# A gated attention and MLP kernel on one core: all steps in a new hand-written order

## The chip, the cores and the metric

The kernel runs on one core of one Trainium2 chip. The metric is device time in microseconds (us). Before the change the median of 3 runs is 445.13 us (444.56 to 445.13).

## What is computed

The output mixes two branches of one input `x` of 2048 rows and 512 columns with a gate per row:

```python
x = A_x
g = _sigmoid((x * gate_w).sum(-1, keepdims=True))
a = _A_ref(x, A_wqkv, A_w_phi, A_wo)
b = _B_ref(x, B_w1, B_b1, B_w2)
return g * a + (1 - g) * b
```

Branch A is linear attention with 32 heads of 16 columns. Queries and keys go through a small matrix per head, then through two softmaxes over the 16 columns (of the value and of its negative), which gives 32 features per head; `kv` is the sum over rows of features of the key times value, `z` the sum of the key features, and the result is `phi_q kv / (phi_q z + 1e-6)`, followed by the matrix `wo`. Branch B is `mish(x w1 + b1) w2` with 1376 hidden columns. All of it is in 32-bit floats; the big products are made of a rounded high part and a low rest (`h` and `l` in the names), three matmuls instead of one.

## The kernel before

The work is cut into steps, each a small Python function filed under a key and a name. The long string `RUN` (line 42) lists all steps, and `run` (L218) calls them in that order. Every instruction is pinned to the program's order, so each engine, and each DMA queue with it, executes its instructions in exactly the order in which the steps stand in `RUN`. An engine that waits for another holds up all that stands behind it on that engine.

The steps have three kinds of keys.

- `A0` to `A7` are eight chunks of 256 rows, of two tiles of 128 rows each. `k`, `q`, `v` and `p1` to `p7` are TensorE products into PSUM (`proj`); for each key tile VectorE takes maximum and minimum per head (`mx`, `mn`, L275), subtracts them (`d0` L285, `d1` L287, into the tile `E`), ScalarE takes the exponential (`E`), VectorE sums (`S`, L291), inverts (`rS`, L299) and scales (`ml`, L302). `kv` (L491) adds to the key-value sums on TensorE and reads `E`. Projected queries are written to DRAM (`st`, tensor `pqd`), and `z` adds up the key features. Behind chunk 7, `zt` and `zf` (L848 to L856) add up `z` across partitions (`zacc`, `zr`); `zs` (L859) writes it to DRAM and `zl` (L863) reads it back, spread over all partitions, as `zb`.
- `S0` and `S1` are the two halves of 1024 rows for the first MLP product. Pairs of hidden tiles are computed with seven products (`p1_n` to `p7_n`, tensor `up`) in place of eight; VectorE forms sums of the weights (`ws`, L687 to L690) and combines the products (`a2` L740, `a3` L743, `a7` L746); ScalarE applies mish (`mA`, `mB`).
- `B0` to `B3` are four blocks of 512 rows. `lq` reads projected queries from `pqd` into one of three `pq` buffers; each of four tiles gets the same softmax features (`mx mn d0 d1 E S rS`), then `T` (L954) multiplies `E` by `zb`, `D` (L958) sums, `m` (L977), `de` (L962), `rd` (L979) and `sc` (L966) make the factor, `es` (L302) scales `E` by it, and `tr` (L969) transposes and stores to DRAM. `mv` reads it back, `nu` multiplies by the key-value sums (`num`), `oh` on ScalarE and `ol` on VectorE (L1012) split the result, `wo` multiplies by the output matrix, `dn` and `df` are the second MLP product (`down`), and `fi` (L1061) mixes and stores.

All matmuls are issued through one helper (`mm`, L118 in the profile), and all activations through another (L138). GpSimd computes the low parts `l` and some sums. ScalarE holds one table of functions at a time; the exponential and mish lie in different tables, and a step `pm` loads the mish table ahead of need.

Of the kernel before, what the change touches and what calls it, by code (L numbers as in the profile page):

```python
# [66 lines left out]
    B0.de0 B0.rd0 S0.p7_2 B0.lo3 B0.hi4 S0.wd_3 B0.sc0 S0.sB1_1 B0.d13 S0.p2_3 B0.es0 S0.a3_2 S0.mB0_2 S0.gl3 S0.c1_3 B1.mn0 S0.sB0_2 S0.a7_2 B0.dn3
    B0.es1 B0.tr1 S0.p6_3 S0.a2_3 S0.p5_3 S0.p4_2 B0.tr0 S0.lg4 B0.lo4 B0.E3 B0.E2 B0.dn4 S0.wa_4 S0.wb_4 S0.p1_4 S0.mA1_2 B1.mx1 B0.T2 S0.c5_3 B0.hi5
    S0.c6_3 B0.lo5 S0.gh4 B0.dn5 B0.D2 B0.S3 B0.rS3 S0.ws_4 B0.T3 B0.D3 S0.p7_3 B0.mv0 B0.hi6 B0.lo6 B1.d10 B1.d00 B0.m3 S0.p2_4 S0.mB1_2 B0.S2
    S0.a7_3 S0.p3_3 S0.a3_3 S0.mA0_3 B0.hi7 S0.wc_4 B1.E0 S0.wd_4 B1.T0 S0.fr1 S0.fh1 B0.dn6 S0.mB1_3 S0.mB0_3 B1.mn1 B0.rS2 B0.m2 S0.n12 S0.p4_3  # L70
    S0.c1_4 S0.sB1_2 B0.de3 B0.lo7 B1.lq2 S0.sB1_3 S0.p5_4 B0.de2 S0.p6_4 B1.D0 B1.d01 S0.mA1_3 S0.h12 S0.a2_4 S0.fl1 B1.mx2 S0.mA0_4 B0.dn7 S0.c6_4
    B0.rd3 S0.p7_4 B0.gl S0.c5_4 B0.rd2 B0.sc2 B0.hi9 B0.hi8 S0.ldo1 S0.p3_4 S0.WH1 B0.sc3 B1.d11 B0.es3 B0.es2 S0.a7_4 S0.sB0_3 S0.o12 S0.uf1 B1.S0
    B0.lo8 B0.dn8 B0.lo9 S0.ldo0 S1.l11 B1.lq3 B0.tr2 B1.E1 B1.S1 B1.mx3 B1.la3 S0.mB1_4 B1.rS1 B1.mn3 B2.lq1 B1.mi0 S0.WL1 B0.tr3 B1.gr S0.a3_4
    S0.p4_4 B1.mn2 S0.WH0 B0.nu0 B0.oh0 S0.gl4 B1.gl B0.dn9 S0.mA1_4 B0.hi10 B0.ol0 B1.rS0 S0.WL0 B0.wo0 B1.hi0 B1.T1 B0.lo10 B1.m0 B0.ge B1.lo0 B1.D1
# [1160 lines left out]
```

## Time and profile before

| | |
|---|---|
| median of 3 runs | 445.13 us |
| the profiled execution's own time | 447.22 us |
| its span, first to last instruction | 445.5 us |
| mean granted TensorE clock | 0.992 |
| busy in the span | PE 427.9, PEld 342.7, DVE 383.1, ACT 258.0, POOL 258.9 us |
| instructions in the span | 7567 |

PE is TensorE, PEld its weight loads, DVE VectorE, ACT ScalarE, POOL GpSimd, SP the engine that issues most DMAs. Matmuls overlap in the profile: a 512-column matmul is listed with about 392 ns, and such matmuls start every 0.23 us when nothing holds them. PE's busy time therefore says little of how much work is left out; the waits, and the time between starts, say more. The two numbers 447.22 and 445.13 are different executions: durations in the text are of the profiled one.

### The profile page before, as it was taken

To read this page: it belongs to the slowest core of one execution; us is meant where nothing else is said; L and a number is where in the kernel's file an instruction comes from. 1 tells how busy PE (TensorE), PEld (TensorE's weight loads), DVE (VectorE), ACT (ScalarE), POOL (GpSimd) and SP (SyncE) were. 2 spreads that over 40 slices of the span, in tenths; PEclk is the share of its full clock that TensorE was granted. 3 is DMA by queue.
4 is the path that set the end of the run, shared out by engine and by line. 5 is a ranking of instruction groups with operands and counts; after the bars stand their busy time and mean duration, and the time that the engine had idled before them with its cause. 6 is when DMAs were issued, how large, how long until landed. Compare 5 with 4: busy or idle time off the path is not lost.

```text
span 445.5 us, 7567 instructions
## 1 busy us (share of the span) xinstructions
PE 427.9 (96%) x2778; PEld 342.7 (77%) x2778; DVE 383.1 (86%) x516; ACT 258.0 (58%) x376; POOL 258.9 (58%) x181
## 2 busy tenths in 40 slices
PE   8999999999999898999799999899999999899996
PEld 7888888888886686778578787688788887678775
DVE  3979798999998988999999999848998799999613
ACT  2556454454546678568588733278595877942331
POOL 2267967887686558476584775475383573641320
PEclk9999999999999899999999999899999999999999
DMA  7804676577985424617656587823343483627552
GB/s 261 307 25 142 167 174 147 153 153 178 232 169 146 143 84 154 200 71 224 187 197 198 190 293 210 270 76 95 96 165 96 150 229 135 173 68 248 169 179 96
DMA packets 52669, 74.06 MB, mean 166 GB/s; under 512 B 8084, under 2 KB 32148, under 8 KB 52632
## 3 DMA queue, kind: packets, MB, share of 16 engines
q1 hardware_dynamic: 50440, 66.36, 46.0%
q0 software_dynamic: 1904, 6.82, 9.1%
q10 hardware_dynamic: 288, 0.39, 0.3%
q8 instruction: 22, 0.36, 0.3%
q14 instruction: 15, 0.12, 0.1%
HBM read 43.53 MB, written 28.85 MB: 162 GB/s over the span
## 4 chain that ended last, share of the span: by engine, by line
PE 59%; DVE 27%; DMA 6%; issue 3%; ACT 2%; SPq 2%; DVEq 0%; ACTq 0%
PE proj L118 26%; PE up L118 15%; PE down L118 10%; PE wo L118 5%; DVE E L302 3%; DVE E L285 3%; DVE T L954 2%; DVE Sm L291 2%; DVE E L969 2%; DVE Dn L977 2%; DMA pq<-pqd 2%; DVE Dn L958 2%; PE kvp L118 2%; DMA wT<-in_wkT_dram 1%; DVE mx L275 1%
## 5 line engine op out<-in xcount | busy, mean ns | idle before, releaser
L118 PE MATMUL down<-w2g,h 128*128 128x512 f32 x316 | 98.4, 392 | 0.0
L118 PEld LDWEIGHTS down<-w2g,h 128*128 128x128 f32 x316 | 58.6, 188 | 14.9 <-issue 2.3
L118 PE MATMUL down<-w2g,l 128*128 128x512 f32 x158 | 61.7, 391 | 1.3 <-POOL l L824 1.3
L824 POOL TENSOR_TENSOR l<-act,h 128x512 fp32r<-128x512 f32 (+1 forms) x24 | 35.4, 1478 | 45.1 <-ACT h L138 20.9
L824 POOL TENSOR_TENSOR l<-actb,h 128x512 fp32r<-128x512 f32 x20 | 26.8, 1344 | 38.9 <-ACT h L138 22.0
L118 PE MATMUL wo<-woh,ohl 128*128 128x512 f32 x128 | 42.6, 399 | 2.6 <-DVE ohl L1012 2.4
L118 PE MATMUL up<-x,w1sh 128*128 128x512 f32 x144 | 39.4, 396 | 5.8 <-ACT act L138 3.1
L138 ACT ACTIVATE E<-E 128x1024 f32<-128x1024 f32 x32 | 33.7, 1057 | 11.8 <-DVE E L285 4.8
L118 PEld LDWEIGHTS up<-x,w1sh 128*128 128x128 f32 x144 | 26.7, 188 | 13.0 <-ACT act L138 4.0
L118 PEld LDWEIGHTS down<-w2g,l 128*128 128x128 f32 x158 | 29.7, 188 | 8.5 <-POOL l L824 2.2
L267 POOL TENSOR_TENSOR xl<-xraw,xh 128x512 fp32r<-128x512 f32 x14 | 19.5, 1452 | 22.9 <-ACT xh L138 19.8
L302 DVE TENSOR_TENSOR E<-E,Sm 128x1024 f32<-128x1024 f32 x18 | 32.1, 1788 | 0.2
L700 POOL TENSOR_TENSOR w1sl<-w1r,w1sh 128x1024 fp32r<-128x1024 f32 x9 | 22.8, 2533 | 15.6 <-ACT w1sh L138 12.1
L118 PEld LDWEIGHTS wo<-woh,ohl 128*128 128x128 f32 x128 | 24.5, 192 | 8.6 <-DVE ohl L1012 2.8
L118 PE MATMUL up<-x,w1d 128*128 128x512 f32 x108 | 27.4, 392 | 2.4 <-DVE act L740 1.8
L138 ACT ACTIVATE h<-actb 128x512 fp32r<-128x512 f32 x20 | 12.6, 629 | 29.1 <-DMA actb<-ab 20.0
L138 ACT ACTIVATE act<-act,b1s 128x512 f32<-128x512 f32 x30 | 21.1, 717 | 13.9 <-DVE act L740 6.9
L628 POOL TENSOR_TENSOR x<-xr,x 128x1024 fp32r<-128x1024 f32 x10 | 24.6, 2464 | 6.6 <-ACT x L138 6.6
L954 DVE TENSOR_TENSOR T<-E,zb 128x1024 f32<-128x1024 f32 x16 | 25.2, 1578 | 3.0 <-DMA zb<-zd 1.7
L118 PE MATMUL proj<-tw,sx 128*128 128x512 f32 x108 | 27.3, 393 | 0.3 <-ACT v L138 0.3
L138 ACT ACT_TABLE_LOAD x21 | 26.9, 1283 | 0.3
L291 DVE TENSOR_REDUCE Sm<-E 128x64 f32<-128x1024 f32 x18 | 21.5, 1197 | 5.7 <-ACT E L138 5.7
(174 smaller groups left out, 1097.5 us busy)
## 6 DMA issues: line engine op xcount, KB each, us to landing
ed<-E SPq DMA_DIRECT2D x16, 512.0 KB, 2.8
eT<-ed SPq DMA_DIRECT2D x64, 128.0 KB, 3.4
za<-E POOLq DMA_DIRECT2D x11, 512.0 KB, 5.7
xr<-in_xT_dram SPq DMA_DIRECT2D x20, 256.0 KB, 4.3
ab<-act SPq DMA_DIRECT2D x20, 256.0 KB, 2.8
actb<-ab SPq DMA_DIRECT2D x20, 256.0 KB, 3.4
pqd<-qs SPq DMA_DIRECT2D x16, 256.0 KB, 2.9
pq<-pqd SPq DMA_DIRECT2D x16, 256.0 KB, 3.5
```

The costliest lines, as they stand in the source:

```text
L118: return pin(nc.tensor.matmul(*a, **k))
L138: return pin(A_.activation(out_, in_, fn, **k))
L267: pin(eng.tensor_sub(xs[c][1][j], kt(rawx[c], SC)[:, 2 * j : 2 * j + 2, :], f32(xs[c][0][j])))
L285: pin(V.tensor_sub(E, hv(src()), d["mx"][:, :, None].to_broadcast([P, H, DH])))
L291: pin(V.tensor_reduce(d["S"], hv(d["E"][:, :]), axis=AX.X, op=ALU.add))
L302: pin(eng.tensor_mul(hv(d["E"][:, :]), hv(d["E"][:, :]), d["S"][:, :, None].to_broadcast([P, 2 * H, DH])))
L628: pin((V if n in LOV else G_).tensor_sub(X[n][:, 1024:], xr[n], f32(X[n][:, :1024])))
L700: pin(G_.tensor_sub(W["sl"], W["r"], f32(W["sh"])))
L824: pin(G_.tensor_sub(U[i]["l"][:n, :], U[i]["a"][:n, :], f32(U[i]["h"][:n, :])))
L954: pin(V.tensor_mul(d["T"], d["E"], B["zb"]))
L958: pin(V.tensor_reduce(d["D"], hv(d["T"][:, :]), axis=AX.X, op=ALU.add))
L969: pin(V.transpose(d["E"][:, :], d["E"][:, :]))
```

## The change

Only the string `RUN` changes: the same steps stand in a new order. It was searched with a replay of the program, in four cases: durations as traced, longer operations, later landings of transfers. No step is added or removed. The mish loads `pm` stand at other places (5 of them before, 1 now), and with the order of exponentials and mish activations the number of table loads on ScalarE goes from 27 to 20. The other engines execute the same instructions in another order. The first two lines of the string show the form:

```diff
-    A0.ldx A2.lx A0.mn0 A0.fq A0.fh1 A0.tA1 A0.fh0 A0.fl0 A0.mx1 A0.tA0 A2.ldx A0.fh2 A0.tB1 A0.fl1 A0.mn1 A0.d10 A0.xh A0.d11 A0.v0 A0.xl A0.tB0
-    A0.v1 A0.fl2 A0.tH1 A1.v1 A0.d01 S0.l11 A0.mx0 A0.d00 A0.tH2 A0.tL2 A0.E0 A0.ve1 A0.S0 A0.fh3 A0.fl3 A1.k0 A1.mx0 A0.tL1 A0.tC3 A0.tH3 A0.tC4
...
+    A1.ldx A0.fq A0.fh0 A0.v0 S0.wr_0 A0.mn0 A0.xh A0.xl S0.l21 A0.mx0 A0.d00 A0.mn1 A0.d10 A0.mx1 A0.d01 A0.E0 A0.fl0 A0.tA0 A0.d11 A0.tA1 A0.fh2
+    A0.tB1 S0.h21 A1.k0 A1.mx0 A0.fl2 A0.tH1 A0.tL1 S0.l11 S0.h11 A0.v1 A0.ve1 A1.mn0 A1.d00 A0.fh1 A0.fl1 A1.d10 A0.fh3 A0.fl3 A0.E1 A2.lx A1.k1
...
```

Three places on VectorE show what moves. Each row is one instruction in the engine's order: line, operation, output<-inputs with their buffer numbers, size.

**Place 1, VectorE, where the second query tile of block 0 comes in (`B0.lq0`).** Before, `pq_164` is the first query tile of block 0 and `pq_213` the second; the first read of `pq_213` (`B0.mn0`) stands ahead of the two subtractions that read `pq_164` last:

```order
L285 TENSOR_TENSOR E_201_1481<-proj_194_1406,mx_207_1508 128x512
L299 RECIPROCAL proj_193_1393<-proj_193_1393 128x64
L275 TENSOR_REDUCE mn_214_1564<-pq_213_1562 128x32
L302 TENSOR_TENSOR E_201_1481<-E_201_1481,proj_193_1393 128x1024
L285 TENSOR_TENSOR E_219_1596<-pq_164_1183,mx_168_1197 128x512
L287 TENSOR_TENSOR E_219_1596<-mn_165_1188,pq_164_1183 128x512
L275 TENSOR_REDUCE mx_221_1603<-pq_213_1562 128x32
L423 TENSOR_TENSOR v_217_1581<-proj_215_1566,v_217_1581 128x512
```

Now, with `pq_185` as the first query tile and `pq_229` as the second:

```order
L285 TENSOR_TENSOR E_215_1580<-pq_185_1352,mx_207_1542 128x512
L287 TENSOR_TENSOR E_215_1580<-mn_201_1480,pq_185_1352 128x512
L302 TENSOR_TENSOR E_197_1443<-E_197_1443,proj_191_1413 128x1024
L423 TENSOR_TENSOR v_210_1557<-proj_216_1583,v_210_1557 128x512
L299 RECIPROCAL proj_183_1332<-proj_183_1332 128x64
L302 TENSOR_TENSOR E_197_1443<-E_197_1443,proj_183_1332 128x1024
L291 TENSOR_REDUCE Sm_221_1623<-E_215_1580 128x64
L628 TENSOR_TENSOR x_219_1605<-xr_126_875,x_219_1605 128x1024
L740 TENSOR_TENSOR act_212_1566<-up_222_1626,act_212_1566 128x512
L429 SCALAR_TENSOR_TENSOR qs_213_1568<-proj_208_1545,qs_213_1568 128x512
L275 TENSOR_REDUCE mx_236_1694<-pq_229_1673 128x32
```

The first read of the second query tile has moved from two rows ahead of the last reads of the first tile to nine rows behind them. On SP, the load of `pq_229` now waits for those last reads, since it takes over the buffer that they free; before, the load of `pq_213` did not wait for VectorE.

**Place 2, VectorE, between the sum of `z` and the first instruction that reads it (`zb`).** `zr` is the sum before it goes through DRAM, `T` the first result of `zb`. Before:

```order
L854 COPY zr_241_1747<-zr_241_1747 32x32 x3
L855 TENSOR_REDUCE zr_241_1747<-zr_241_1747 32x32
L856 STREAM_TRANSPOSE zr_241_1747<-zr_241_1747 32x32
L291 TENSOR_REDUCE Sm_257_1834<-E_219_1596 128x64
L426 TENSOR_TENSOR qs_223_1608<-proj_203_1492,qs_223_1608 128x512
L687 TENSOR_TENSOR w1r_233_1716<-w1r_233_1716 128x2x128
L688 TENSOR_TENSOR w1r_233_1716<-w1r_233_1716 128x2x128
L689 SCALAR_TENSOR_TENSOR w1r_233_1716<-w1r_233_1716 128x2x128
L690 TENSOR_TENSOR w1r_233_1716<-w1r_233_1716 128x2x128
L954 TENSOR_TENSOR T_264_1868<-E_219_1596,zb_252_1816 128x1024
```

Now, the first 12 rows from the same point:

```order
L854 COPY zr_237_1696<-zr_237_1696 32x32 x3
L855 TENSOR_REDUCE zr_237_1696<-zr_237_1696 32x32
L856 STREAM_TRANSPOSE zr_237_1696<-zr_237_1696 32x32
L426 TENSOR_TENSOR qs_214_1576<-proj_202_1488,qs_214_1576 128x512
L687 TENSOR_TENSOR w1r_206_1536<-w1r_206_1536 128x2x128
L688 TENSOR_TENSOR w1r_206_1536<-w1r_206_1536 128x2x128
L689 SCALAR_TENSOR_TENSOR w1r_206_1536<-w1r_206_1536 128x2x128
L690 TENSOR_TENSOR w1r_206_1536<-w1r_206_1536 128x2x128
L628 TENSOR_TENSOR x_241_1759<-xr_44_354,x_241_1759 128x1024
L285 TENSOR_TENSOR E_215_1580<-pq_229_1673,mx_236_1694 128x512
L869 TENSOR_TENSOR km_253_1808<-kvp_92_628,mask_110 128x256
L870 STREAM_TRANSPOSE km_253_1808<-km_253_1808 128x256
```

Six rows stood between the last instruction on `zr` and the first `T`. Now it is 21 rows, of which the first nine are shown, and the first tile that `T` reads is another: `B0.T0` in place of `B0.T1`.

**Place 3, VectorE, the last combination in the second half of the MLP (`S1.a7_4`).** In both orders `act<-up` at L746 is the last row of the fence, the last combination `S1.a7_4`; L743 a few rows ahead is `S1.a3_4`. TensorE's product `S1.p4_4` waits for L746. Before:

```order
L275 TENSOR_REDUCE mn_596_3716<-pq_575_3589 128x32
L275 TENSOR_REDUCE mx_601_3738<-pq_600_3736 128x32
L962 SCALAR_TENSOR_TENSOR den_603_3745<-Dn_560_3510 128x32
L740 TENSOR_TENSOR act_588_3675<-up_583_3631,act_588_3675 128x512
L299 RECIPROCAL Sm_590_3691<-Sm_590_3691 128x64
L743 TENSOR_TENSOR act_597_3718<-up_589_3684,act_597_3718 128x512
L979 RECIPROCAL den_603_3745<-den_603_3745 128x32
L966 TENSOR_TENSOR Sm_576_3593<-Sm_576_3593,den_603_3745 128x64
L746 SCALAR_TENSOR_TENSOR act_598_3726<-up_580_3610,act_598_3726 128x512
```

Now:

```order
L966 TENSOR_TENSOR Sm_582_3615<-Sm_582_3615,den_594_3704 128x64
L287 TENSOR_TENSOR E_586_3647<-mn_551_3458,pq_549_3452 128x512
L302 TENSOR_TENSOR E_477_3043<-E_477_3043,Sm_582_3615 128x1024
L743 TENSOR_TENSOR act_595_3712<-up_591_3667,act_595_3712 128x512
L275 TENSOR_REDUCE mn_606_3782<-pq_567_3541 128x32
L302 TENSOR_TENSOR E_477_3043<-E_477_3043,Sm_558_3512 128x1024
L954 TENSOR_TENSOR T_608_3788<-E_586_3647,zb_250_1795 128x1024
L958 TENSOR_REDUCE Dn_609_3790<-T_608_3788 128x64
L746 SCALAR_TENSOR_TENSOR act_593_3681<-up_557_3499,act_593_3681 128x512
```

Between L743 and L746 stood two short rows; now it is four rows, three of them over 1024 columns or its sums. Between the combination `S1.a3_3` and `S1.a7_4` there are now 19 instructions on VectorE, and on TensorE, between the products `S1.p3_3` and `S1.p4_4`, 54 matmuls of 512 columns and the 32 short ones of `B2.nu0`.

More of the change, by code (lines that the diff above doesn't have):

```diff
@@ L67 @@
[L67 to L74, printed above, removed]
```

108 lines of the change are left out of this document (58 added, 50 removed).

## The prediction

> **What bounds the kernel now.** I read the page first: busy times, then the chain that ended last.
>
> ```profile
> PE 427.9 (96%) x2778; PEld 342.7 (77%) x2778; DVE 383.1 (86%) x516; ACT 258.0 (58%) x376; POOL 258.9 (58%) x181
> PE 59%; DVE 27%; DMA 6%; issue 3%; ACT 2%; SPq 2%; DVEq 0%; ACTq 0%
> ```
>
> PE is nearly full, and its 2778 matmuls are the same ones after the change. So a new order can win only what PE loses now: waits, and time at a lower clock. It can lose much more. A quarter of the chain lies on DVE, so DVE is the second engine to follow. Next comes the view of waits for PE (engine, tile and line, releaser: total us, times, longest).
>
> ```profile
> PE up L118 <- DVE act L740: 3.7, 2, 2.0
> PE up L118 <- ACT act L138: 3.1, 2, 2.0
> PE wo L118 <- DVE ohl L1012: 2.4, 1, 2.4
> PE down L118 <- POOL l L824: 1.3, 2, 0.7
> ```
>
> These four rows hold 10.5 us. To see where they lie I cut the span into windows: length, busy us and instructions of PE, PEld, DVE, ACT and POOL, granted clock, DMA share, GB/s.
>
> ```profile
> 130.00:168.20 38.20, 35.87 (x266) 28.37 (x267) 33.30 (x47) 25.13 (x40) 23.62 (x16) 0.96 0.51 137
> 168.20:280.10 111.90, 103.31 (x530) 80.88 (x528) 110.16 (x138) 73.51 (x106) 75.08 (x44) 1.00 0.60 192
> 280.10:356.00 75.90, 75.61 (x353) 61.03 (x354) 61.54 (x90) 51.97 (x76) 41.63 (x26) 0.98 0.41 132
> ...
> 147.00:150.40 3.40, 3.40 (x10) 2.63 (x9) 3.40 (x3) 1.55 (x2) 0.87 (x1) 0.50 0.28 100
> 280.10:283.50 3.40, 3.10 (x7) 2.48 (x8) 3.33 (x5) 0.00 (x0) 3.40 (x3) 0.50 0.83 279
> ```
>
> From 130.0 to 280.1 us, 150.1 us in all, DVE is busy for 33.30 + 110.16 = 143.5 us and PE for 35.87 + 103.31 = 139.2 us: **this stretch is DVE's**, and PE idles in it for 10.9 us. It begins where the last products of the queries and keys meet the second query tile (place 1), and ends where `B1.wo0` waits for DVE's `B1.ol0`. Behind it PE is busy for 75.61 of 75.90 us and DVE idles for 14.4. Before 130 us PE hardly waits, and I find no place in the new order where it would.
>
> **The change part by part.** The new order's stretch between the same two points holds 180 DVE instructions where 183 stood, and 6 matmuls fewer; both have moved ahead of it. Starts of matmuls show what six are worth, and the end of the stretch is in the same view (start, us, instruction, idle before it):
>
> ```profile
> 277.20 0.62 PE L118 MATMUL down<-w2g,h 128*128 128x512 f32 x2
> 277.65 0.39 PE L118 MATMUL down<-w2g,l 128*128 128x512 f32 x1
> 280.39 0.79 PE L118 MATMUL wo<-woh,ohl 128*128 128x512 f32 x1 [2.35 <-DVE ohl L1012]
> ```
>
> Two matmuls take 277.65 - 277.20 = 0.45 us, so 0.23 each, and six 1.4 us. Three mean DVE instructions of the stretch are 3 x 143.5 / 185 = 2.3 us; so DVE gets ahead by at most 0.9 us of PE. By kind the three are shorter than the mean, and I cost this at **nothing**, with 0 to -0.9 for the range. DVE therefore still sets the end, and what counts is its idle time in the stretch, 150.1 - 143.5 = 6.6 us. Two waits hold most of it, and the chain gives the transfers behind them (start, us, what):
>
> ```profile
> DVE mn L275 <- DMA pq<-pqd: 2.2, 1, 2.2
> DVE T L954 <- DMA zb<-zd: 1.7, 1, 1.7
> ```
>
> ```profile
> 130.12 7.86 DMA pq<-pqd
> ...
> 161.91 1.77 DMA zd<-zr
> 163.69 4.40 DMA zb<-zd
> ```
>
> *Place 1.* The read of the second query tile stands now behind nine other rows. Its load on SP does wait for the last reads of the first tile, a wait that is new, but eight DVE instructions stand between those reads and its first reader; at the stretch's mean of 0.776 us they take 6.2 us, and 7.9 with the durations that they had as traced (`x` and `E` products among them), against a landing of 7.86. Behind that load on SP stand a weight load, a gate row, a store and the load of the fourth query tile, whose first reader stands over ten DVE rows further back, which covers them too. I take the wait as gone, -2.2, with 0 as the other end.
>
> *Place 2.* The write and the read of `z` take 1.77 + 4.40 = 6.2 us. Six DVE instructions covered 4.4 us of it; 21 instructions at 0.776 cover 16. The wait goes: -1.7. What is late next there is `z` itself: its sum over partitions (`zt`) now stands close behind GpSimd's two last additions.
>
> ```profile
> L480 POOL TENSOR_TENSOR zacc<-zacc,E x2: 2401/2914/3427, 144.4 to 152.7; 128x1024 f32<-128x1024 f32 x2
> ```
>
> That tile's row (least, median, longest ns) bounds a new wait by 0 and one addition, 3.4 us. By the work that stands ahead of each on its engine, DVE reaches `zt` about 1 us before GpSimd ends: +1.0. Both places: -2.2 - 1.7 + 1.0 = **-2.9** us (0 to -3.9). PE has 10.9 us of idle time there, so it can follow.
>
> *The clock.* Directly behind the wait of 2.35 us at 280.4 stands a window at a granted clock of 0.50, for 3.4 us; it costs 1.7. The earlier one, at 147, also stands behind a wait of PE, but inside the stretch where DVE is the later engine: nothing is won there. If DVE ends 2.9 us earlier, the wait at `wo` falls to about nothing and the dip with it: **-1.7**.
>
> The Trainium skill, page "TensorE: Matmul & The Clock Gate", section "HAM oscillation — how this bites in real kernels", has the clock drop only behind an idle gap of more than about 3.4 us. The trace differs, 0.50 behind 2.35 us. By that rule the dip would have another cause and stay, and 1.7 us would have to be added to the sum.
>
> *Place 3.* `S1.p4_4` on PE waits for `S1.a7_4` on DVE. From `S1.a3_3`, which itself waits for the product `S1.p3_3`, to `S1.a7_4` there are 21 instructions, both included. Their groups (form xcount | busy us, mean ns | idle before):
>
> ```profile
> L302 DVE TENSOR_TENSOR E<-E,Sm 128x1024 f32<-128x1024 f32 x18 | 32.1, 1788 | 0.2
> L954 DVE TENSOR_TENSOR T<-E,zb 128x1024 f32<-128x1024 f32 x16 | 25.2, 1578 | 3.0 <-DMA zb<-zd 1.7 <-ACT E L138 1.3
> ...
> L285 DVE TENSOR_TENSOR E<-pq,mx 128x512 f32<-128x512 f32 x16 | 20.1, 1255 | 0.0
> ...
> L958 DVE TENSOR_REDUCE Dn<-T 128x64 f32<-128x1024 f32 x16 | 19.1, 1201 | 0.2
> ...
> L302 DVE TENSOR_TENSOR E<-E,proj 128x1024 f32<-128x1024 f32 x14 | 17.0, 1213 | 0.2
> L287 DVE TENSOR_TENSOR E<-mn,pq 128x512 f32<-128x512 f32 x16 | 13.9, 868 | 0.0
> L977 DVE TENSOR_TENSOR Dn<-Dn,Sm 128x64 f32<-128x64 f32 x16 | 11.1, 702 | 0.1
> ...
> L285 DVE TENSOR_TENSOR E<-proj,mx 128x512 f32<-128x512 f32 x16 | 10.8, 684 | 0.1
> ...
> L299 DVE RECIPROCAL Sm<-Sm 128x64 f32<-128x64 f32 x18 | 9.6, 540 | 0.2
> ...
> L966 DVE TENSOR_TENSOR Sm<-Sm,den 128x64 f32<-128x64 f32 x16 | 6.6, 420 | 0.4
> ...
> L979 DVE RECIPROCAL den<-den 128x32 f32<-128x32 f32 x16 | 5.4, 343 | 0.2
> ...
> L962 DVE SCALAR_TENSOR_TENSOR den<-Dn 128x32 f32<-128x32 f32 x16 | 2.9, 187 | 0.2
> ```
>
> Two each of `E<-E,Sm`, `E<-mn,pq`, `Dn<-Dn,Sm`, `Sm<-Sm` (L299), `Sm<-Sm,den`, `den<-den` and `den<-Dn` are 2 x (1.788 + 0.868 + 0.702 + 0.540 + 0.420 + 0.343 + 0.187) = 9.7; one each of `T`, `D` (L958) and `E<-pq,mx` are 1.578 + 1.201 + 1.255 = 4.0; three combinations and one minimum, all 512 columns, at the 0.684 of `E<-proj,mx` are 2.7. That is 16.4 us. Rows of DVE overlap a little:
>
> ```profile
> 138.61 1.21 DVE L302 TENSOR_TENSOR E<-E,proj 128x1024 f32<-128x1024 f32 x1
> 139.74 2.97 DVE L285 TENSOR_TENSOR E<-pq,mx 128x512 f32<-128x512 f32 x1
> 142.63 0.68 DVE L287 TENSOR_TENSOR E<-mn,pq 128x512 f32<-128x512 f32 x1
> ```
>
> 1.21 us are listed where the next starts after 1.13: 0.08 less. Twenty times this is 1.6, which leaves 14.8. PE meanwhile has 54 matmuls x 0.23 = 12.4 us and the short ones of `num`:
>
> ```profile
> 431.24 1.02 PE num L118 x32
> ```
>
> 13.4 in all. PE waits for 14.8 - 13.4 = **+1.4** us at `S1.p4_4`, where it has no wait to speak of now.
>
> *The tail.* Of PE's two waits for `l` (1.3 us) one goes: the second `l` stood behind this row on POOL, and now stands ahead of it. Minus **0.6**; the other stays. The seven table loads that fall away are off the path (ACT is busy for 58%) and count nothing, with 0 to -0.6 for the other wait for `l`.
>
> ```profile
> 374.76 2.40 POOL L586 TENSOR_TENSOR wol<-raw,woh 128x1024 fp32r<-128x1024 f32 x1
> ```
>
> The sum is -2.9 - 1.7 + 1.4 - 0.6 = **-3.8 us**. The profiled execution took 447.22 us, so it would take 443.4; it lies 2.1 above the median of the runs, to which I carry the difference over: 445.13 - 3.8 = **441.3 us**.
>
> **The rivals.** *Meetings with GpSimd.* The sum holds only if DVE's durations stay on average what they were, and these are no property of a step. `E<-E,proj` and `E<-E,Sm` do the same work on the same 1024 columns, the one with an input in PSUM, the other with both in SBUF: 1213 against 1788 ns. The tile's rows show why the means differ:
>
> ```profile
> L302 DVE TENSOR_TENSOR E<-E,Sm x18: 1178/1226/3425, 36.0 to 418.8; 128x1024 f32<-128x1024 f32 x18
> ...
> L954 DVE TENSOR_TENSOR T<-E,zb x16: 1154/1294/2317, 168.2 to 404.5; 128x1024 f32<-128x1024 f32 x16
> ```
>
> The median is as short as the other's; a few take up to 3.4 us. In the trace these long ones end when a GpSimd operation ends. The excess over a free operation is (1788 - 1213) x 18 = 10.4, (1255 - 684) x 16 = 9.1, (868 - 684) x 16 = 2.9 and, for `T` against 1213, 5.8: 28.2 us on 66 instructions. I put half of it, 14.1 us, into the DVE stretch, an estimate by the length of the stretch and GpSimd's share in it (98.7 us of 150.1). The new order draws all these meetings anew.
>
> The Trainium skill, page "SBUF — State Buffer", section "SBUF: two separate sides", says that the pair of ports that DVE and GpSimd share is an exclusive lock held for a whole instruction, for DVE operations with two SBUF inputs. The rows agree, 1213 against 1788 ns. By it the duration belongs to the meeting, and a sum of durations as traced, like mine, says nothing of what the meetings of the new order cost.
>
> *Slower* is this: between place 1 and `B1.ol0` the meetings cost half as much again, +7.1 us on the engine that sets the end, and the time is 441.3 + 7.1 = 448.4. It decides from 3.8 us on, 27% more of the 14.1. For it: DVE is the later engine for 150 us with nothing in reserve, and GpSimd's order has changed too. Against: the trace of before is one draw already, and not a lucky one. *Faster still* is the other sign: 30% less, -4.2, so 437.1.
>
> *Given back in S1.* DVE's 21 instructions include the two `E<-E,Sm` and a `T`. If one and the `T` are as long as the longest of their rows, PE waits 3.425 - 1.788 + 2.317 - 1.578 = 2.4 us longer, 3.8 in all; after 2.35 us the clock was halved before, so another 1.7 is due: 441.3 + 4.1 = 445.4, no change. For it: `S1.p4_4` has no cover. Against: it takes two long ones among three.
>
> **How the numbers follow.** The forecast, 441.3, has a chance of 0.45, with a range of its own from 439 to 444.2: it takes in a pq wait that stays (+2.2), a wait for GpSimd at `zt` of 3.4 in place of 1.0 (+2.4), a dip that stays (+1.7, by itself about 0.1 of the 0.45, which is the page's case at 443.0), and the ends at -0.9 and -0.6. More meetings, 448.4: 0.27. Fewer, 437.1: 0.15. Given back in S1, 445.4: 0.13. From 436.5 to 449.0 about 0.1 is left out above and 0.07 below. 0.2% is 0.9 us, about what a measurement of this kernel can tell from no change: faster (under 444.2) 0.45 + 0.15 = 0.60, same 0.13, slower 0.27.
>
> **What would show it.** Right: no wait of DVE for `pq` or `zb`; the wait of PE for `ohl` under 1 us and a full clock behind it; one new wait of PE for L746 of about 1.4 us near the end of S1, and one wait for `l`. The mean of `E<-E,Sm` near 1.8 us and of `E<-pq,mx` near 1.25 would show that the meetings cost what they did; above 2.2 and 1.5 the first rival holds. Wrong: waits of PE before 130 us, a long wait of DVE for `zacc`, or an `S1` wait beyond 3 us. That the order doesn't do what it says would show as the old waits at the old places.

## The result, and the profile after

The changed kernel took a median of 442.26 us (441.73 to 443.59, 7 runs) against 445.96 us (444.56 to 447.25, 7 runs) for the kernel before: a ratio of 0.9922, 95% interval 0.9900 to 0.9944, that is 3.5 us less. In a second measurement, beside other kernels, the ratio was 0.9891 (0.9850 to 0.9933). The forecast was 441.3 us and a gain of 3.8. The ratios in this document leave out executions that took over 1.5% longer than the fastest of their kernel; the medians take in all.

The profiled execution took 442.8 us, with a span of 440.8, which is 4.7 less than in the profile before. Its busy times and the engines of its chain:

```profile
PE 425.7 (97%) x2778; PEld 340.8 (77%) x2778; DVE 375.9 (85%) x516; ACT 248.5 (56%) x369; POOL 260.4 (59%) x181
PE 65%; DVE 21%; DMA 4%; issue 3%; ACT 3%; POOL 1%; SPq 1%; DVEq 0%; POOLq 0%; ACTq 0%
```

VectorE's share of the chain fell from 27% to 21%, and its busy time by 7.2 us, although it executes the same 516 instructions. PE's waits:

```profile
PE down L118 <- POOL l L824: 2.6, 3, 1.5
PE wo L118 <- DVE ohl L1012: 1.7, 1, 1.7
PE up L118 <- DVE E L302: 1.1, 1, 1.1
PE warm L118 <- DVE ones L188: 1.1, 1, 1.1
PE up L118 <- DVE act L740: 1.1, 2, 0.8
PE fuse L118 <- issue: 1.0, 1, 1.0
PE down L118 <- ACT h L138: 1.0, 2, 0.8
PE up L118 <- ACT act L138: 0.8, 1, 0.8
PE num L118 <- ACT act L138: 0.8, 1, 0.8
PE proj L118 <- DVE qs L429: 0.3, 1, 0.3
```

They add up to 11.5 us; the ten rows of before add up to 14.1. The long waits for the MLP's combinations (3.7) and activations (3.1) are down to 1.1 and 0.8; in their place stand shorter ones that were not there, for `l`, `h` and the fused weights. The places of the prediction now lie at 130.3 us (place 1), 275.7 us (`B1.wo0`) and 370.9 us (`S1.p4_4`). By stretch:

```profile
130.30:168.20 37.90, 35.66 (x273) 27.52 (x272) 37.30 (x51) 26.91 (x41) 26.88 (x17) 1.00 0.47 131
168.20:275.70 107.50, 101.13 (x514) 79.67 (x513) 102.74 (x134) 66.06 (x99) 71.31 (x41) 0.98 0.63 201
275.70:356.20 80.50, 80.50 (x382) 64.97 (x382) 66.12 (x91) 53.05 (x80) 49.20 (x31) 1.00 0.41 131
```

VectorE's stretch is 145.4 us long in place of 150.1, and VectorE is busy in it for 37.30 + 102.74 = 140.0 us in place of 143.5. So it idles for 5.4 us in place of 6.6. Behind it PE is busy without a gap, as before. `B1.wo0` itself now waits for nothing: VectorE starts `B1.ol0` at 273.7 us, and PE comes to `B1.wo0` at 275.7 straight from its own products. The 1.7 us for `ohl` in the list above belong to an earlier `wo`, at 247.6 us. What VectorE waits for in the stretch:

```profile
DVE ohl L1012 <- ACT ohl L138: 2.2, 1, 2.2
DVE T L954 <- ACT E L138: 1.5, 2, 1.1
```

The rows for `pq` and `zb` are gone, and none for `zacc` has come. In their place VectorE waits 2.2 us for ScalarE's half of the split of `num`, where it waited 0.3 before. That wait stands right ahead of `B1.ol0`, and what is late there is PE's `num` (271.9 to 272.9 us), behind PE's own waits for `h` and `l`. So in the changed kernel the end of the stretch is no longer VectorE's alone.

### The profile page after: what moved, and what is told of

Read it like the earlier page. It is cut to its first block, busy times and chain, and to the rows that moved or that the text cites. A ratio compares the mean times of both kernels' runs of the same rounds, so it can differ in the third digit from the quotient of the medians.

```text
span 440.8 us, 7559 instructions
## 1 busy us (share of the span) xinstructions
PE 425.7 (97%) x2778; PEld 340.8 (77%) x2778; DVE 375.9 (85%) x516; ACT 248.5 (56%) x369; POOL 260.4 (59%) x181
## 4 chain that ended last, share of the span: by engine, by line
PE 65%; DVE 21%; DMA 4%; issue 3%; ACT 3%; POOL 1%; SPq 1%; DVEq 0%; POOLq 0%; ACTq 0%
PE proj L118 26%; PE down L118 15%; PE up L118 13%; PE wo L118 7%; DVE T L954 2%; DVE Dn L958 2%; DVE E L302 2%; PE kvp L118 2%; DVE Sm L291 2%; DVE E L285 1%; DMA actb<-ab 1%; DVE E L287 1%; DVE E L969 1%; ACT L138 1%; PE num L118 1%
## 5 line engine op out<-in xcount | busy, mean ns | idle before, releaser
L118 PE MATMUL down<-w2g,l 128*128 128x512 f32 x158 | 62.6, 396 | 2.6 <-POOL l L824 2.6
L824 POOL TENSOR_TENSOR l<-actb,h 128x512 fp32r<-128x512 f32 x20 | 29.4, 1476 | 41.0 <-ACT h L138 18.3
L118 PE MATMUL wo<-woh,ohl 128*128 128x512 f32 x128 | 41.0, 390 | 1.7 <-DVE ohl L1012 1.7
L700 POOL TENSOR_TENSOR w1sl<-w1r,w1sh 128x1024 fp32r<-128x1024 f32 x9 | 23.1, 2567 | 15.3 <-ACT w1sh L138 14.1
L302 DVE TENSOR_TENSOR E<-E,Sm 128x1024 f32<-128x1024 f32 x18 | 28.8, 1603 | 0.1
L628 POOL TENSOR_TENSOR x<-xr,x 128x1024 fp32r<-128x1024 f32 x10 | 25.7, 2580 | 2.2 <-ACT x L138 1.5
L138 ACT ACTIVATE act<-up 128x512 f32<-128x512 f32 x30 | 17.6, 593 | 13.9 <-PE up L118 10.8
L118 PE MATMUL wo<-wol,ohl 128*128 128x512 f32 x64 | 24.9, 389 | 0.0
```

Of the source, the lines that this page charges most:

```text
L118: return pin(nc.tensor.matmul(*a, **k))
L138: return pin(A_.activation(out_, in_, fn, **k))
L302: pin(eng.tensor_mul(hv(d["E"][:, :]), hv(d["E"][:, :]), d["S"][:, :, None].to_broadcast([P, 2 * H, DH])))
L628: pin((V if n in LOV else G_).tensor_sub(X[n][:, 1024:], xr[n], f32(X[n][:, :1024])))
L700: pin(G_.tensor_sub(W["sl"], W["r"], f32(W["sh"])))
L824: pin(G_.tensor_sub(U[i]["l"][:n, :], U[i]["a"][:n, :], f32(U[i]["h"][:n, :])))
```

## The experiments

Three theories were open. **A**, the prediction's: VectorE sets the end of the stretch before `B1.wo0`, and the two waits for transfers are what the new order takes off it. **B**: the time is won in the tail. **C**: it is won because VectorE's long operations meet GpSimd's at luckier moments; 3.4 of the 4.7 us could be that by the windows.

| kernel | median us, runs | ratio to before (95%) |
|---|---|---|
| premid | 447.53, 10 | 0.9978 (0.9934 to 1.0021) |
| midtail | 454.59, 4 | 1.0105 (1.0024 to 1.0186) |
| tail | 447.76, 10 | 0.9949 (0.9901 to 0.9997) |
| b_waits | 446.11, 10 | 0.9943 (0.9906 to 0.9979) |
| z_before | 432.63, 4 | 0.9639 (0.9590 to 0.9688) |
| z_after | 431.24, 4 | 0.9617 (0.9575 to 0.9660) |
| a_T1 | 450.42, 10 | 1.0063 (1.0028 to 1.0098) |
| a_plus | 440.64, 4 | 0.9825 (0.9784 to 0.9866) |
| after_again | 442.82, 6 | 0.9891 (0.9850 to 0.9933) |
| b_w1 | 446.83, 12 | 0.9973 (0.9929 to 1.0016) |
| b_w2 | 446.25, 12 | 0.9941 (0.9909 to 0.9974) |
| a_plus2 | 445.08, 12 | 0.9940 (0.9909 to 0.9972) |

Each group of four was run beside runs of the kernel before on its chip, whose medians there were 448.63, 447.70 and 447.52 us.

### Halves of the two orders: premid, midtail, tail

Each is one list of steps up to a point and the other list's remaining steps behind it, in their own order.

```
premid:   new order up to B1.wo0, then old order of the rest
midtail:  old order up to A6.kv,  then new order of the rest
tail:     old order up to B1.wo1, then new order of the rest
```

> The new order up to the first product for `B1.wo0`, the old order behind it. Theory A (the time is won in the stretch of VectorE before `B1.wo0`): 3 to 4.5 us faster than the kernel before, ratio 0.990 to 0.993, with the waits for the tile `l` and for `E` in the tail back at the old places (about 1.8 us). Rival B (the time is won in the tail, by fewer table loads and earlier `l`): under 1.5 us faster, ratio above 0.9965.

> The old order up to `A6.kv` (about 134 us), the new order behind it. Theory A: the first 130 us give nothing, so the time is that of the changed kernel, 3.5 to 5 us under the kernel before (ratio 0.989 to 0.992). If the first part counts (its new wait of about 1 us among the fused weights, or an earlier start of the stretch), it differs from the changed kernel by 1 us or more.

> The old order up to `B1.wo1` (about 283 us), the new order behind it. Theory A: only the tail's waits can go, so 0.5 to 1.2 us faster than the kernel before (ratio 0.997 to 0.999), and the wait for `ohl` and the half clock behind it stay. Rival B: 2.5 us or more faster (ratio under 0.9945).

None came out as theory A had it. midtail is slower than either order: at the seam PE waits 5.0 us for one row of VectorE, `A7.ml0` (`up` for `E`, L302), where it waits 1.1 in the changed kernel. By the ratios alone premid is as B had it, above 0.9965, and A's 0.990 to 0.993 lies just outside its interval; tail, at 0.9949, lies between the two forecasts, and its interval takes in both. So the halves by themselves speak for B rather than for A. Why premid, with the new order up to `B1.wo0`, shows so little of the gain can be looked up. It has the same instructions in the same order there as the changed kernel, so the two traces can be laid side by side. PE waits for a mish activation at 197.8 us in premid and at 194.3 in the changed kernel:

```profile
PE up L118 <- ACT act L138: 3.4, 1, 3.4
```

3.4 us here, 0.8 in the changed kernel. In premid, VectorE ahead of that place (start, length), then GpSimd:

```profile
189.05 2.32 DVE L302 TENSOR_TENSOR E<-E,Sm 128x1024 f32<-128x1024 f32 x1
191.29 2.88 DVE L285 TENSOR_TENSOR E<-pq,mx 128x512 f32<-128x512 f32 x1
```

```profile
188.96 1.33 POOL L824 TENSOR_TENSOR l<-act,h 128x512 fp32r<-128x512 f32 x1 [3.46 <-PE down L118]
190.31 3.32 POOL L700 TENSOR_TENSOR w1sl<-w1r,w1sh 128x1024 fp32r<-128x1024 f32 x1
```

And in the changed kernel, the same four instructions:

```profile
187.74 1.22 DVE L302 TENSOR_TENSOR E<-E,Sm 128x1024 f32<-128x1024 f32 x1
188.87 1.78 DVE L285 TENSOR_TENSOR E<-pq,mx 128x512 f32<-128x512 f32 x1
```

```profile
187.97 2.13 POOL L824 TENSOR_TENSOR l<-act,h 128x512 fp32r<-128x512 f32 x1 [3.79 <-PE down L118]
190.06 2.85 POOL L700 TENSOR_TENSOR w1sl<-w1r,w1sh 128x1024 fp32r<-128x1024 f32 x1
```

In premid GpSimd's `l` starts 0.09 us ahead of VectorE's `E<-E,Sm`, which then takes 2.32 us and ends 1.08 after `l` has ended. In the changed kernel VectorE starts 0.23 us ahead, takes 1.22, and it is `l` that is stretched, to 2.13. With the row behind it, 0.32 us of difference in who comes first costs VectorE 1.10 + 1.10 = 2.2 us, and PE's wait is 2.6 longer. So the rival of the meetings is real at this size, within one and the same order. It is not all that premid lost: its span is 6.6 us over the changed kernel's. PE also waits 1.2 us for GpSimd's `sx` ahead of this place, 1.5 for an `l` at the seam, and 0.9 more in the old order's tail. A hybrid of two orders has a seam and draws its meetings anew, so halves like these cannot tell the theories apart; an edit of one or two steps is the better tool.

### The two waits alone: b_waits, b_w1, b_w2

The kernel before, with the first reader of the second query tile moved behind three rows of VectorE (b_w1), the first reader of `zb` behind three others (b_w2), and both (b_waits):

```diff
-  ... B0.lq0 B0.mn0 A7.p2 A7.ml0 ... B0.d01 S0.gl1 S0.h3 B0.d11 B0.mx0 ...
+  ... B0.lq0 A7.p2 A7.ml0 ... B0.d01 S0.gl1 S0.h3 B0.d11 B0.mn0 B0.mx0 ...
-  ... S0.wc_2 B0.T1 B0.mx2 S0.a2_1 B0.D1 B0.lo2 ... S0.p1_2 B0.d02 S0.lg2 ...
+  ... S0.wc_2 B0.mx2 S0.a2_1 B0.d02 B0.T1 B0.D1 B0.lo2 ... S0.p1_2 S0.lg2 ...
```

> The kernel before with only the two waits for transfers taken out: `B0.mn0` moved behind `B0.d11`, and `B0.T1` behind `B0.d02`. VectorE should lose about 3.5 of the 3.9 us of its waits for `pq` and `zb`. Theory A, in the form of the prediction (these waits are what sets the end of the stretch): 3 to 5.5 us faster than before, and no half clock at 280 us. Rival C (GpSimd's meetings set VectorE's time and are drawn anew): the waits are gone from the trace, but the sum of VectorE's long operations changes by as much or more, and the time moves by less than 1.5 us or the wrong way.

> The kernel before with place 1 alone: `B0.mn0` moved behind `B0.d11`, so that VectorE no longer waits for `pq`. Theory A: its 2.2 us come off the end of the stretch, 1 to 2.5 us faster (ratio 0.9945 to 0.998). If the later wait for `zb` takes the gain back (the transfer of `z` starts from GpSimd and not from VectorE): under 0.9 us.

> The kernel before with place 2 alone: `B0.T1` moved behind `B0.mx2`, `S0.a2_1` and `B0.d02`. Theory A: about 1.6 us of wait for `zb` come off, 0.8 to 2 us faster (ratio 0.9955 to 0.998); with b_w1 it adds up to what both together gave, 2.5 us.

b_waits is 0.57% faster than before, some 2.5 us, with two steps moved. In its profile the span is 441.6 us, 3.9 less than before. Its busy row, and all that VectorE still waits for from 130 to 276 us:

```profile
PE 426.0 (96%) x2778; PEld 340.4 (77%) x2778; DVE 382.9 (87%) x516; ACT 257.9 (58%) x376; POOL 257.8 (58%) x181
```

```profile
DVE ohl L1012 <- ACT ohl L138: 0.8, 1, 0.8
DVE E L287 <- PE kvp L118: 0.4, 1, 0.4
DVE T L954 <- ACT E L138: 0.4, 1, 0.4
```

VectorE is busy for 382.9 us, as before (383.1): here nothing came from luckier meetings. The two waits are gone, and `B1.ol0` starts at 275.6 us in place of 279.7, so the 3.9 us of waits arrive there whole. That is theory A without help from C, and without help from B, since the tail is untouched. The size is smaller than A had it: 2.5 us by the ratio, where 3 to 5.5 were expected. The profiled execution is the fastest of its ten, 2.8 us under their median and with no half clock in it, so its 3.9 us are not the gain of a usual one. One edit alone gives about half in the profile: `B1.ol0` starts at 277.4 us in b_w1 and 277.2 in b_w2. In the times the two don't add up: by the ratios b_w1 gives 1.2 us, with no change inside its interval, and b_w2 2.6, as much as both together. Single edits of 1 to 2 us are at the limit of what these runs can tell.

### One wait put back: a_T1

The changed kernel with one step moved.

```diff
-  ... A7.zl S0.wc_1 ... S0.mB0_0 B0.T1 B0.S0 ...
+  ... A7.zl B0.T1 S0.wc_1 ... S0.mB0_0 B0.S0 ...
```

> The changed kernel with one step moved: `B0.T1`, the first reader of `zb` then, stands 6 rows behind the last row on `zr`, as the first `T` did before. Theory A: VectorE waits for `zb` again, about 4 us by the landing seen in the changed kernel, and the time is 2.5 to 4.5 us over the changed kernel's (ratio to the kernel before 0.998 to 1.003). If VectorE were not what sets the end of the stretch: under 1 us over it (ratio under 0.9945).

1.0063 against 0.9922 and 0.9891 for the changed kernel: 6 us or more, and not 2.5 to 4.5. VectorE shows why, with two long waits where one was expected (and a third, of 1.2 us, for `pq`):

```profile
164.58 1.23 DVE L954 TENSOR_TENSOR T<-E,zb 128x1024 f32<-128x1024 f32 x1 [4.76 <-DMA zb<-zd]
...
179.02 1.23 DVE L954 TENSOR_TENSOR T<-E,zb 128x1024 f32<-128x1024 f32 x1 [4.62 <-POOL w1sl L700]
```

The first is the wait that was put back. The second is one of buffers: `T` shares three buffers with the raw weights `w1r` (in the code both are taken with the tag `tx`), and with `T` allocated earlier the next `T` has to wait until GpSimd's `w1sl` has read the `w1r` ahead of it. That the two come from one move follows from the code and the releaser in the row; it was not tried apart. PE waits 4.8 us for VectorE's `km` behind the first of them, so here a wait of VectorE reaches PE nearly whole.

### GpSimd's reads taken out: z_before, z_after

Both kernels with nine kinds of subtractions on GpSimd replaced by a fill of the same tile, so that these low parts are left out of the result.

```diff
-  pin(G_.tensor_sub(U[i]["l"][:n, :], U[i]["a"][:n, :], f32(U[i]["h"][:n, :])))
+  pin(G_.memset(f32(U[i]["l"][:n, :]), 0.0))
```

> The kernel before, with nine kinds of GpSimd subtractions (most of its low parts, L824, L700, L681, L682, L559, L586, L790, L368, L535) replaced by a fill with zeros of the same tile, which reads nothing: these low parts are left out of the result. It is read against its pair z_after. If GpSimd's reads of SBUF stretch VectorE's operations: the mean of `E<-E,Sm` falls from 1788 to under 1350 ns and the time by 5 us or more. If not, the mean stays over 1700 ns.

> The changed kernel with the same subtractions replaced by fills. Theory A (the new order wins by waits for transfers that no longer stand in VectorE's way): z_after stays 2.5 to 4.5 us faster than z_before. Theory C (it wins by luckier meetings of VectorE and GpSimd): the two are within 1.2 us of each other.

z_before is some 15 us faster than the kernel before, z_after 11 to 13 faster than the changed kernel. In z_before, the group, the busy row and the two waits of VectorE:

```profile
L302 DVE TENSOR_TENSOR E<-E,Sm 128x1024 f32<-128x1024 f32 x18 | 23.7, 1320 | 0.2
```

```profile
PE 423.9 (98%) x2778; PEld 341.7 (79%) x2778; DVE 345.6 (80%) x516; ACT 257.9 (60%) x376; POOL 158.3 (37%) x181
```

```profile
DVE T L954 <- DMA zb<-zd: 3.1, 1, 3.1
DVE mn L275 <- DMA pq<-pqd: 1.8, 1, 1.8
```

The mean of `E<-E,Sm` falls from 1788 to 1320 ns and VectorE's busy time by 37.5 us: without GpSimd's reads its operations on two SBUF inputs are short. That it is the reads, and not only that the fills are shorter, is in the same trace: 15 of the 50 rows `E<-E,Sm`, `T` and `E<-pq,mx` start while a fill is under way, and none of them is long. The difference of the two orders shrinks to 1.4 us by the medians and 1.0 by the ratios, on both sides of the 1.2 that C had been given and under A's 2.5. Still it decides neither, for a reason that I should have seen: with 37.5 us less to do VectorE has slack, and the two waits, which are still there (4.9 us), cost PE only one wait of 1.8. It does show on what theory A rests: **VectorE sets the end of the stretch by the time that its meetings with GpSimd cost it**, and only so long does a wait on VectorE cost much. The fills also no longer wait for ScalarE's `h`, so the gain is not all the meetings'.

### Better orders: a_plus, a_plus2

The changed kernel with five steps moved where its trace has PE waiting.

```diff
-  A7.rS0 B0.d01 B0.d11 A7.p2 A7.p7 A7.ml0 ... S0.o3 S0.p2_0 S0.a2_0 ... A7.a7
+  A7.rS0 A7.ml0 B0.d01 B0.d11 A7.p2 A7.p7 ... S0.p2_0 S0.a2_0 ... A7.a7 S0.o3
-  B1.sc1 B1.dn0 B1.sc0 B1.es1 S1.h11 B1.la2 B0.oh1 B1.d02 B0.ol1 ... B1.la5 ... B1.tr1 B1.la6
+  B0.oh1 B0.ol1 B1.sc1 B1.dn0 B1.sc0 B1.es1 S1.h11 B1.la2 B1.d02 ... B1.la5 B1.la6 ... B1.tr1
```

a_plus2 has three more:

```diff
-  B1.E2 ... B1.D2 S1.o11 B1.hi3 B0.wo3 B1.hi4 B1.es0 B1.hi2 B1.lo2
+  B1.hi2 B1.hi3 B1.E2 ... B1.D2 B1.lo2 S1.o11 B0.wo3 B1.hi4 B1.es0
```

> The changed kernel with five steps moved where its own trace shows PE waiting: `A7.ml0` ahead of `B0.d01`, `S0.o3` behind `A7.a7`, `B0.oh1` and `B0.ol1` ahead of `B1.sc1`, `B1.la6` right behind `B1.la5`. Each takes away a wait of PE that VectorE or a landing set (1.1, 1.0, 1.7 and 2.3 us, and the half clock behind the last, 1.7). If PE's waits are local: 4 to 6 us faster than the changed kernel (ratio to the kernel before 0.978 to 0.984). Theory A (VectorE's sum sets the end of the stretch, and a wait that goes here comes back later): 0.5 to 3 us faster (ratio 0.985 to 0.991).

> The changed kernel with the five moves of a_plus and three more: `B1.hi2` and `B1.hi3` ahead of `B1.E2` on ScalarE, `B1.lo2` ahead of `S1.o11` on GpSimd, where a_plus waited for 2.0 and 1.0 us and then ran 6.8 us at half clock. If that stretch is PE's own: 3 to 6 us under a_plus (ratio to the kernel before 0.969 to 0.976). Theory A: VectorE's next due product takes the place, 0 to 2.5 us under a_plus (ratio 0.977 to 0.9825).

> The changed kernel again, as the measure for the three kernels beside it: ratio to the kernel before 0.990 to 0.994.

a_plus is the fastest order here, 440.64 us and 0.9825, though its execution still ran 6.8 us at half clock. The ratio lies in the range that I gave to local waits; against the changed kernel's own, 0.9922 and 0.9891, it is 0.7 to 1% or 3 to 4 us, and by the medians 1.6 to 2.2, so whether part of the waits came back later is not decided by it. It beats the kernel before clearly; its interval (0.9784 to 0.9866) still touches that of the changed kernel's second measurement (0.9850 to 0.9933). a_plus2 moves three more steps, and both forecasts for it missed: it is slower than a_plus by 1.2%, and than the changed kernel measured beside it by 0.5%. PE's next wait in its profile, and VectorE and GpSimd ahead of it:

```profile
PE wo L118 <- DVE io L1061: 3.5, 1, 3.5
```

```profile
245.24 2.88 DVE L285 TENSOR_TENSOR E<-pq,mx 128x512 f32<-128x512 f32 x1
...
250.38 2.33 DVE L954 TENSOR_TENSOR T<-E,zb 128x1024 f32<-128x1024 f32 x1
```

```profile
244.20 3.37 POOL L628 TENSOR_TENSOR x<-xr,x 128x1024 fp32r<-128x1024 f32 x1
...
249.22 2.41 POOL L612 TENSOR_TENSOR xr<-xr,xr 128x1024 f32<-128x1024 f32 x1
```

`B1.lo2` ahead of `S1.o11` moved two long GpSimd operations onto an `E<-pq,mx` and a `T`, which took 2.88 and 2.33 us; in a_plus the same two took 0.68 and 1.22. Those 3.3 us are not the loss, though: other rows were long in a_plus there, and VectorE reaches `io` only 1.3 us later. PE's wait of 3.5 is not the loss either. Both kernels issue the same matmuls in the same order, so one product can be set against itself, first of a_plus, then of a_plus2:

```profile
259.11 0.39 PE L118 MATMUL wo<-woh,ohl 128*128 128x512 f32 x1
```

```profile
256.47 0.50 PE L118 MATMUL wo<-woh,ohl 128*128 128x512 f32 x1 [3.54 <-DVE io L1061]
```

Up to here the three moves won 2.6 us, and the wait of 3.5 only shows that PE was free earlier. The loss comes behind it. First PE runs a window at half clock from 257.0 us, which costs 1.7. Then there is VectorE's next `Dn<-Dn,Sm`, in a_plus and then in a_plus2:

```profile
256.77 0.94 DVE L977 TENSOR_TENSOR Dn<-Dn,Sm 128x64 f32<-128x64 f32 x1
```

```profile
258.03 2.38 DVE L977 TENSOR_TENSOR Dn<-Dn,Sm 128x64 f32<-128x64 f32 x1
```

With the 1.3 us from above, VectorE ends the transposed `E` that follows 2.7 us later. The transfers that stand behind its store on SP start later too, and PE waits 1.9 us for an `h` that hangs on them; that `down` starts at 273.8 us, against 271.1 in a_plus. From 274.0 us a second window at half clock costs 1.7 more, and the last product starts 5.0 us later than in a_plus. The moves had been judged by PE's waits alone; what came of them on VectorE and for the clock cost more. Which of the three did it was not tried apart.

## Why the prediction was right, and where it was not

The total was right, -3.8 us against -3.5 measured, and so was the main mechanism: the two waits for transfers were what could be taken off the late engine. That the sum came so near is in part luck: two costs that had been added, 1.0 at `zt` and 1.4 at `S1.p4_4`, did not come, and others stood in for them. By PE's losses in the two profiles the terms compare so, the stretch with the wait at its end:

| term | forecast us | measured us |
|---|---|---|
| before 130 us | 0 | +1.0 (`fuse`) |
| stretch before `B1.wo0`, PE's waits | -2.9 | -2.6 (11.2 to 8.6) |
| half clock | -1.7 | -1.7 (two stretches, then one) |
| `S1.p4_4` | +1.4 | 0 |
| tail | -0.6 | -1.0 (1.8 to 0.8) |
| sum | -3.8 | -4.3 of 4.7 in the spans |

*Before 130 us.* The wait for the fused weights (`fuse`, 1.0 us) need not be the new order's: one of 1.1 stands in b_w2 and one of 0.6 in tail, which have the old order there.

*Places 1 and 2.* Both waits went, as forecast, and b_waits shows that they are worth 3.9 us on VectorE and some 2.5 us of time by themselves. The term that failed is the new wait at `zt`, +1.0: GpSimd ended its last addition at 148.1 us and VectorE came to `zt` at 150.9. What I did not foresee is the wait of 2.2 us for ScalarE's `ohl` and more of `T` for `E`: VectorE's idle time fell by 1.2 us and not by 2.9.

*The meetings.* "DVE's durations stay on average what they were" failed, to the good side: VectorE was busy for 3.4 us less in the stretch. The group of the eight `E<-E,Sm` there went from 16.9 to 14.0 us, the next lines being of before and of the changed kernel; other groups moved both ways (`Dn<-Dn,Sm` from 7.1 to 4.4, `den<-Dn` from 1.4 to 4.8):

```profile
L302 DVE TENSOR_TENSOR E<-E,Sm 128x1024 f32<-128x1024 f32 x8 | 16.9, 2121 | 0.0
```

```profile
L302 DVE TENSOR_TENSOR E<-E,Sm 128x1024 f32<-128x1024 f32 x8 | 14.0, 1754 | 0.0
```

So the rival of fewer meetings came true beside the forecast, at -3.4 where it had -4.2, and made up for the idle time that stayed. It is no mere accident of one execution (the second profile of the changed kernel has VectorE busy for 375.9 us again), but premid shows that the same order can lose it. The rule of the Trainium skill that the prediction weighed (page "SBUF — State Buffer", section "SBUF: two separate sides": who starts first holds the shared ports for the whole instruction) agrees with the pairs of rows under premid, 1.22 against 2.32 us. One reading of the prediction was not exact: the long rows do not end when the GpSimd operation ends, but about one free row's length later, as the last section shows.

*The clock.* At its own place the step came true: `B1.wo0` no longer waits, and no half clock stands behind it. But the rule that it used, that a long wait of PE brings the half clock, did not hold, and the -1.7 of the sum owes something to luck. The half clock at 147 us went too, from which I expected nothing; the new wait of 1.7 us for `ohl`, at 247.6, has no half clock behind it; and one stands at 267.5 us, behind two new waits of 0.8 and 1.5 us for `h` and `l`. The rule of the Trainium skill that the prediction set against it (page "TensorE: Matmul & The Clock Gate", section "HAM oscillation — how this bites in real kernels": an idle gap of over about 3.4 us) does not agree either: no wait of PE in the two profiles is longer than 2.4 us, and three half clocks stand in them. What holds is told at the end.

*Place 3.* Mis-sized. VectorE's first 20 rows took from 357.7 to 368.8 us, and with `S1.a7_4` all 21 take 11.8 us in place of 14.8. Of the 3.0 us, 1.3 are the two `E<-E,Sm` and the `T`, which drew 1.22, 1.42 and 1.21 us and not the means of 1.79 and 1.58; 1.1 are the two `Dn<-Dn,Sm`, 0.35 us together and not 1.4; and the one `E<-pq,mx` gives 0.6:

```profile
360.34 0.35 DVE L977 TENSOR_TENSOR Dn<-Dn,Sm 128x64 f32<-128x64 f32 x2
...
362.70 1.22 DVE L302 TENSOR_TENSOR E<-E,Sm 128x1024 f32<-128x1024 f32 x1
...
365.03 1.42 DVE L302 TENSOR_TENSOR E<-E,Sm 128x1024 f32<-128x1024 f32 x1
366.37 1.21 DVE L954 TENSOR_TENSOR T<-E,zb 128x1024 f32<-128x1024 f32 x1
...
369.96 0.69 DVE L746 SCALAR_TENSOR_TENSOR act<-up,act 128x512 f32<-128x512 f32 x1 [1.12 <-PE up L118]
```

Then VectorE waited for PE and not PE for VectorE. A mean over rows that meet GpSimd and rows that don't is the wrong price for a single row: a row of 1024 columns took 1.2 us where it met nothing, and up to 3.4 where it did.

*Table loads.* Costed at nothing; the tail, where the profile has fewer of them (10 and not 14), won 1.0 us where -0.6 was forecast. No run takes them apart from the rest. That theory B is not the whole is shown by b_waits and a_T1, which leave the tail as it was and win 2.5 us and lose 6. How much the tail gives is open: 1.0 us by PE's losses, 2.3 by the ratio of the kernel tail, with an interval from 0.1 to 4.4.

What stays open is how the 3.5 us divide: b_waits gives 2.5 by waits alone, with an interval from 0.9 to 4.2, the meetings have up to 3.4 on VectorE, and the tail 1.0 by PE's losses. The waits are shown by an edit of their own in the kernel before; the shares of the three in the new order are not settled by the runs.

## What to carry to other kernels

Find the engine that is late stretch by stretch, and count its idle rows there: two waits of 2 us for transfers, taken off by moving one reader each behind three rows that were ready anyway, were worth 2.5 us, where a new order of 1200 steps brought 3.5. But look at what else the late engine waits for before you price a move: where VectorE's operations with two inputs in SBUF meet GpSimd's, as here, a change in who starts first can cost the late engine as much as such a wait (2.2 us for 0.32 us in premid). And test a large reordering by moving single steps; halves of two orders bring in a seam and new meetings of their own. When a variant comes out slower, set the same instruction of both traces side by side before you blame the longest wait: in a_plus2 the engine was ahead where it waited longest.

## What the runs showed of the hardware

**VectorE and GpSimd.** In the 14 traces of this study I followed the 50 rows `E<-E,Sm`, `T` and `E<-pq,mx` of each, all with two inputs in SBUF. Free, they take about 1.2 us at 1024 columns and 0.7 at 512. All 246 that took over 1.33 or 0.8 us end 1.08 to 1.09 us (1024 columns) or 0.55 to 0.56 us (512) after the end of a GpSimd operation that reads SBUF; the two premid rows above are of this kind. Of the 414 rows that started with no such operation under way none was long, the 24 among them that started during a fill (in z_before and z_after) included. So a long row is a row that stood still until GpSimd had ended, although the profile lists it as busy.

**TensorE's clock** is not halved by the length of a wait. The half-clock stretches are 3.413 us long, or two of these in a row (in b_w2, a_plus and tail), and start on a fixed grid of that step within an execution: in the kernel before at 146.992 and 280.112, which is 39 steps apart. Windows laid on that grid (length, PE busy, ..., granted clock), of the kernel before: the one ahead of each half clock, and two around its wait of 2.0 us that ends at 223.2:

```profile
143.58:146.99 3.41, 1.43 (x7) 0.88 (x6) 3.41 (x6) 1.80 (x3) 2.54 (x1) 1.00 0.02 2
...
276.70:280.11 3.41, 1.34 (x6) 0.76 (x5) 3.38 (x4) 2.38 (x4) 2.73 (x2) 1.00 0.37 154
222.10:225.50 3.40, 2.32 (x10) 1.93 (x11) 3.37 (x8) 3.40 (x6) 0.72 (x1) 1.00 0.79 208
218.67:222.08 3.41, 2.48 (x11) 1.70 (x10) 3.41 (x3) 0.16 (x1) 2.07 (x1) 1.00 0.68 230
```

And of b_w1, around a wait of PE of 3.1 us, longer than any in the kernel before:

```profile
273.21:276.62 3.41, 1.89 (x9) 1.20 (x7) 3.38 (x4) 2.35 (x5) 2.76 (x2) 1.00 0.38 154
276.62:280.04 3.42, 1.89 (x8) 1.58 (x9) 3.35 (x6) 0.00 (x0) 3.42 (x3) 1.00 0.51 163
280.04:283.45 3.41, 3.41 (x16) 2.83 (x16) 3.34 (x7) 0.00 (x0) 0.37 (x1) 1.00 0.91 255
```

The wait of 3.1 us lies half in one window and half in the next, PE is busy for 1.89 us in each, and the clock stays whole. The wait of 2.0 us ahead of 147 and that of 2.35 ahead of 280 lay within one window each or nearly so, PE was busy for 1.43 and 1.34 us of it, and the next window ran at half clock. The wait of 2.0 at 222 fell into two windows, and the clock stayed whole. Over the 14 traces of this study, between 20 and 420 us and from windows at full clock, all 17 windows in which PE idled for 1.76 us or more (half of a window is 1.71) were followed by a half clock, and none of those under 1.70; of six in between, two were. The grid lies elsewhere in each execution, so the same wait can cost 1.7 us in one and nothing in the next: of the seven executions of the changed kernel five have a mean clock of 0.996, which is one half clock, and two 0.999 and 1.0. This is likely part of the spread from run to run. Another part is likely the meetings with GpSimd: with the fills, four runs of z_before lay within 1.7 us, where the kernel before spread over 6.2 in 13 runs on that chip. That was not tried apart from the number of runs.
